# The k-kernel generation of a two-layer attention and state-space block: another hand-written order, an earlier zero fill, a later load and two earlier projections

## The chip, the cores and the metric

The kernel runs on one core of a Trainium2 chip. The metric is the device time of one execution in microseconds (us). A core has five engines with their own instruction streams: PE (TensorE, matrix products), DVE (VectorE), ACT (ScalarE), POOL (GpSimd) and SP (SyncE, which here only issues DMA transfers). Each engine works through its stream in order and waits on semaphores. All DMAs but one are issued from SP, so SP's stream is also an order of transfers.

## The reference, cut to what matters

```python
x = x + A(layernorm(x))      # attention, 32 heads of 16, 8 keys back at distance 2
x = x + B(layernorm(x))      # S4: long convolution with a generated kernel K
x = x + A(layernorm(x))      # the same weights again
x = x + B(layernorm(x))

# A: qkv = x @ wqkv; logits over 8 dilated keys; softmax; o = attn @ v; o @ wo
# B: dt = exp(log_dt); P = exp(dt * (A_re + i A_im) * l), l = 0..2047
#    K = real(sum_n C * P * dt * B)          # 512 x 2048, bf16 positions
#    y = irfft(rfft(u, 4096) * rfft(K, 4096))[:2048] + u * Dskip
```

x is 2048 x 512 in bf16, the state size N is 128. K depends on the inputs alone and is the same in both B layers.

## The kernel before, in words

**Stages.** The program has six stages, each handing over to the next on the engines without a barrier: the generation of K together with the front of the first A layer (`k_gen`, L883, until about 119 us), the rest of the first A layer (`LayerA.core`, L307, until about 209 us), the first B layer by a two-level Fourier transform (`FftB`), the second A layer, the second B layer, and the stores of the output, spread over the last stage.

**`k_gen`.** K is built from powers of z = exp(dt*A). Eleven squarings give z to the power 1, 2, 4, ... 2048; DVE multiplies two sets of tables out of them (`B_t` for coarse positions, `A_t` for fine ones, in four chunks of channels), PE contracts the tables over the 128 states into PSUM, ACT copies them to `kgs`, and SP stores them to `kd_dram` in 48 small DMAs (`k_store`, L1147). Into the gaps goes the front of attention: the statistics of x, its normalisation, its transposes, the projections to q and k, and the first three logit products of block 0. The order of all this is written out by hand: `ORDERK` (L44) is a string of 376 letters, each letter is a list of small closures, and the loop at L1211 calls the next closure of the letter. The tile framework keeps that order on DVE, ACT, PE and SP (`manual_schedule`). The letters that the prediction speaks of:

- s: ACT squares both parts of the current power (L959). i: DVE finishes the next power, in turn `double` (L963) and `differ` (L966).
- b: ACT casts a power into `B_t` (L975) or into the fine table `pow_t` (L973, and its negative at L978). c: SP copies a plane of `pow_t` (L981).
- C: DVE forms the coefficient dt*B*C (eight products). M: DVE builds `B_t` (`bmul`, L995).
- T, U: DVE builds `A_t`, chunks 0 and 2 by T, 1 and 3 by U (L1093). The first U also frees the small buffers of the generation (`stage_two`, L1088), so its copy (L1099) waits for everything that reads them.
- a, l, W, y, z: statistics of x rows (ACT), four small DVE steps per block of x, of which the last (L1056) needs the power -1/2 that POOL makes (W, L1060), then the normalisation on ACT (y, L158) or DVE (z).
- t, e, k, q, K, Q: transposes and projections on PE, their copies out of PSUM on ACT (L1072, L1084). d, E, w, on SP: loads of x blocks 2 and 3, the shifted copies of k (L253), the stores of the twiddle table `w2` (L652).
- p, x: the contraction on PE (L1136), its copy on ACT (L1144). X, Z, g: logit products of block 0 on DVE, their sums on PE, masks.

At the start SP issues the loads of A, B and C, the first block of x, the weights for k and q (`front_w`, L213), the second block of x, and the zero fill of `w2_dram` (`zero`, L645): 4 MB from a 128 x 256 tile of zeros, in pieces of 512 bytes. The fill has to be complete before w2 is stored over it.

**After the letters.** The two `k_store` calls come last in SP's stream of this stage, behind the E copies and the load of the v weights (`load_wv`, L258), and ahead of the loads of the output weights, of Dskip, and of the first shifted copy of v.

**`core` of layer 0.** Nine slots (block 0 from its fourth product on, blocks 1 and 2) each do one product q*k on DVE (`mult`, L289) and its head sums on PE (`lsum`, L298). The projections still missing, 16 of v and 4 of q, are dealt out over the slots at an even rate:

```python
449	            slots = [(0, ft) for ft in range(nprod, NDT)] + [(q, ft) for q in (1, 2) for ft in range(NDT)]
450	            free = 2 if l else 0
451	            per, acc = len(projs) / (len(slots) - free - 0.5), 0.0
```

After v blocks 14 and 15 a shifted copy of v is made by two DMAs (L353, L354), one for the even, one for the odd blocks; x is loaded again behind the second. Then 16 steps follow, each with one weighted sum attn*v: the product on DVE (`pv_mult`, L394), its sum on PE (L407), the output projection (L413). Events hang on these steps (`ev`, L1328): at ("o", n) after step n, at ("p", n) within it. Among them: the load of each half of K from `kd_dram` in 18 DMAs (`k_half_load`, L1305); the four sines of the second twiddle table, each with its store to `g2_dram` (`sines`, L678), which use the buffer `kp` as scratch; `k_half_fix` and `k_part` (L1311, L1315), which copy K into the same `kp`, quarter by quarter, so quarter j of the first half waits until store j has been read out; and the load of w2 (L539).

Of the kernel before, what the change touches and what calls it, by code (L numbers as in the profile page):

```python
# [15 lines left out]
BF16 = mybir.dt.bfloat16  # L16
# [4 lines left out]
P = 128  # L21
# [8 lines left out]
EXP_LN = "natural_log_exp_and_others"  # L30
# [11 lines left out]
DQT = 8  # L42
NQT = DQG // DQT
ORDERK = """  # L44
iCsbisCbiiCbiMsGMiaCCsibCbcGisCMCbaMTibTiasMcbTMiaibbTsMbTaacMcTiMTMaTaiTsbilGTGlilbTWTlGsiibMMy
MMMyaGTyGGbMyGMisMacTtMMiaaaMtdaMaMaGaebMasliMlMqleMWMqialMyMyQMGwqyyMqQbkMkMaMMKtUgkUaUkkUTUaaU
UatUKUppkklkdeUlKxUqqlUpW3UKl3UxQpTUeTkqkqTy3yyyTt3KTTQElqtTxkqlkQxTKpkqkWTKpxkqTlTxTezepzQTpkkU
zUUKkzUKTkkkUtUkTKekkUKtxqKqQUUkpeUqkqUExxpUKUXxUpUxkpQkUEUKUkkxUUkKpxpXkXKUpXXxpZXxZgZx
"""
ORDER0 = """  # L50
KA KD KA KD KA KA KD KA KD KA KD kA KD KA KA kD kA kD kA UA KD UA UA UD UA kD UA
# [111 lines left out]
class LayerA:  # L163
# [143 lines left out]
    def core(self, x_sb, u, lnp, ev=None, nprod=0):  # L307

        tc, nc, lnst, l = self.tc, self.nc, self.lnst, self.layer
# [3 lines left out]
        ev = ev or {}  # L313
# [8 lines left out]
        with ExitStack() as c2:  # L322
            self.prp = c2.enter_context(tc.tile_pool(name=f"a{l}_prod", bufs=2, reuse_waits="tile"))
            big = c2.enter_context(tc.tile_pool(name=f"a{l}_big", bufs=1, reuse_waits="tile"))
            v = big.tile([P, NA + 14, D], BF16, name="v_ext")
# [119 lines left out]
            projs = [(q_proj, 1, ft) for ft in range(NDT)] if 1 not in self.qT else []  # L445
# [2 lines left out]
            projs += [(v_proj, a) for a in vs[6:]]  # L448
            slots = [(0, ft) for ft in range(nprod, NDT)] + [(q, ft) for q in (1, 2) for ft in range(NDT)]
            free = 2 if l else 0  # L450
            per, acc = len(projs) / (len(slots) - free - 0.5), 0.0

            def proj(n):
                nonlocal acc
# [118 lines left out]
def build_b_consts(nc, cpool, tmp, w2_dram):  # L573
# [6 lines left out]
    aidx = iota_f32(nc, tmp, "aidx", 16, step=4096)  # L580
    d4i = iota_f32(nc, tmp, "d4i", 4)
    nc.gpsimd.iota(base[:], pattern=[[16, EQ], [4096, 16]], base=8, channel_multiplier=0)
    zt = tmp.tile([P, 256], BF16, name="w2_zero")
    nc.gpsimd.memset(zt[:], 0.0)
    t_i = tmp.tile([P, 8], I32, name="pk_t")
    nc.vector.tensor_scalar(t_i[:, 0:1], pi_i[:], 63, 2, ALU.bitwise_and, ALU.logical_shift_right)
# [56 lines left out]
                                dmask_m.unsqueeze(1).to_broadcast([P, 32, 4]), ALU.mult)  # L643

    def zero():  # L645
        nc.sync.dma_start(w2_dram.rearrange("p e c -> p (e c)").rearrange("p (n x) -> p n x", x=256),
                          zt[:].unsqueeze(1).to_broadcast([P, P * P // 256, 256]))

    def w2_store():
        for s in range(4):  # L650
# [6 lines left out]
    steps += [lambda nm=nm, t=t: f1_sine(nm, t) for nm, t in zip(("F1c", "F1s"), f1t)]  # L657
    steps += [w2_sine] + [lambda name=name: w_sine(name) for name, offs in wps]
    return C, zero, steps, w2_store, [lambda name=name: w_mask(name) for name, offs in wps]


# [4 lines left out]
def build_g2(nc, tmp, p21, g2_dram, room):  # L666

    s8 = 2.0 * math.pi / 65536 * SIN_SHRINK
    own = tmp.tile([P, 2, 8 * P], I32, name="g2_i")
    gi = [own[:, 0], own[:, 1], *(room[:, (2 + h) * 16 * P:(3 + h) * 16 * P].bitcast(I32) for h in range(2))]  # L670

    def indices(h):
        for k, bias in enumerate((16384.0, 32768.0)):
            g = gi[h][:, k * 4 * P:(k + 1) * 4 * P]
            nc.gpsimd.iota(g.rearrange("p (a m) -> p a m", m=P), pattern=[[8, 4], [128, P]], base=32 * h, channel_multiplier=0)
            nc.gpsimd.tensor_scalar(g, g, p21, bias, ALU.mult, ALU.add)

    def sines(h):  # L678
        gs = room[:, h * 8 * P:(h + 1) * 8 * P]
        nc.scalar.activation(gs, low16(gi[h]), ACT.Sin, scale=s8)  # L680
        nc.sync.dma_start(g2_dram[:, :, h * 4:(h + 1) * 4, :], gs.rearrange("p (k a m) -> p k a m", k=2, a=4))

    return indices, sines
# [199 lines left out]
def k_gen(tc, nc, ident, ins, kd, la, x_v, lnst, b_consts):  # L883
# [4 lines left out]
    with ExitStack() as ctx:  # L888
# [16 lines left out]
        def x_load(b):  # L905
            xb[b] = la.fp.tile([P, 4, D], BF16, name="x_blk")
            nc.sync.dma_start(xb[b][:], x_v[:, b * 4:(b + 1) * 4, :])
# [4 lines left out]
        for name in ("A_im", "A_re", "B_re", "B_im", "C_re", "C_im"):  # L912
            raw[name] = sp.tile([P, 4, N], BF16, name="raw_" + name)
            nc.sync.dma_start(raw[name][:], ins[name].rearrange("(t p) n -> p t n", p=P))
            if name == "A_re":
                x_load(0)
        la.front_w()
        x_load(1)
        C, zero, steps, w2_store, masks = b_consts(sp)
        zero()  # L920
        nc.vector.memset(Bt[:, 0, :, 0, :], 1.0)
        nc.vector.memset(Bt[:, 1, :, 0, :], 0.0)

# [236 lines left out]
        def first_logits():  # L1160
            pr = {}

            def mult(ft):
                if ft == 0:
                    pr[0] = tab[0].tile([P, 2, W, 4, P], BF16, name="A_pr", tag="A_t")
                    pr[1] = tab[0].tile([P, W, 4, P], BF16, name="A2_pr", tag="A_t2")
                la.mult(0, ft, pr[0][:, ft] if ft < 2 else pr[1][:])

            for ft in range(3):
                yield lambda: la.front_ext(3, "dve", ft)  # L1170
                yield lambda: mult(ft)
# [13 lines left out]
        def calls(f, *args):  # L1185
            return [lambda a=a: f(*a) for a in args]

        def chain(*fs):
# [18 lines left out]
            p=calls(product, *((c, j) for c in range(NCH) for j in range(CH // 8))),  # L1207
            x=calls(produced, *((c, j) for c in range(NCH) for j in range(CH // 8))), X=first_logits(), Z=calls(lsum, (0,), (1,), (2,)))
# [15 lines left out]
def k_load(tc, nc, kr, kd, ds_):  # L1224
    l = np.arange(2048, dtype=np.float32)
    m = bf16_round_np(l).astype(np.int64).reshape(128, 16) - 16 * np.arange(128)[:, None]
    nc.sync.dma_start(kr[0:16], kd[0:256, ds_].rearrange("(p a) d -> p a d", a=16))
    n = 1
    for o, (p0, p1, base) in enumerate(((16, 32, 256), (32, 64, 384), (64, 128, 512))):
        s = 2 << o  # L1230
        blk = m[p0:p1]
        assert (blk == blk[0:1]).all() and (blk % s == 0).all()
        row = [int(v) for v in blk[0]]
        np_ = p1 - p0
        q = 16 // s
        runs = []
        for v in range(0, 17, s):
            c = [a for a in range(16) if row[a] == v]
            assert c == list(range(c[0], c[-1] + 1))
            runs.append((v // s, c[0], len(c)))  # L1240
        for (t, a0, cnt) in runs:
            rows = kd[base + t:base + t + (np_ - 1) * q + 1:q, ds_]
            nc.sync.dma_start(kr[p0:p1, a0:a0 + cnt, :],
                                                              rows.unsqueeze(1).to_broadcast([np_, cnt, D // 2]))
            n += 1
# [3 lines left out]
def kernel(  # L1249
# [16 lines left out]
    nc = tc.nc  # L1266
    cpool = ctx.enter_context(tc.tile_pool(name="consts", bufs=1))
    dram = ctx.enter_context(tc.tile_pool(name="dram", bufs=1, space=bass.MemoryType.DRAM))
    w2_dram = dram.tile([P, P, P], BF16, name="w2_dram")
# [16 lines left out]
    la = LayerA(tc, nc, consts, lnst, A_wqkv, A_wo, 0, xnT, 2)  # L1286

    with tc.manual_schedule(engines=MAN):
        C = k_gen(tc, nc, consts["ident"], ins, kd, la, x_v, lnst, lambda sp: build_b_consts(nc, cpool, sp, w2_dram))
# [15 lines left out]
    def k_half_load(h):  # L1305
        hs = slice(h * 256, (h + 1) * 256)
        kr = krp.tile([P, NA, D // 2], BF16, name=f"k_rl{h}")
        k_load(tc, nc, kr, kd, hs)
        krs[h] = kr

    def k_half_fix(h):  # L1311
        kr = krs[h]
        nc.vector.tensor_tensor(kr[0:1, 0, :], kr[0:1, 0, :], dsk[:, h * 256:(h + 1) * 256], ALU.add)

    def k_part(h, j):  # L1315
        cp = nc.scalar.copy if j % 2 == 0 else nc.vector.tensor_copy
        cp(kp[:, h * 64 + j * 16:h * 64 + (j + 1) * 16, :, :],
           krs[h][:, :, j * 64:(j + 1) * 64].rearrange("p a (q r) -> p q a r", r=4))

    def x_load():  # L1320
        for b in range(4):
            nc.sync.dma_start(x_sb[:, b * 4:(b + 1) * 4, :], x_v[:, b * 4:(b + 1) * 4, :])

    with tc.tile_pool(name="ctmp_g2", bufs=1) as g2tmp, tc.manual_schedule(engines=MAN):
        gx, gs = build_g2(nc, g2tmp, C["p21"], g2_dram, kp[:].rearrange("p q a r -> p (q a r)"))
        G = lambda f, h: lambda: f(h)
        K = lambda h, j: lambda: k_part(h, j)
        ev = {("v", 1): [x_load], ("o", 1): [lambda: k_half_load(0)], ("o", 2): [G(gs, 0)], ("o", 4): [lambda: k_half_load(1)],  # L1328
              ("m", 1, 0): [lambda: nc.scalar.preload_act_table_set(EXP_LN)],
              ("m", 0, 3): [G(gx, h) for h in range(4)],  # L1330
              ("p", 3): [G(gs, 1)], ("p", 4): [G(gs, 2)], ("p", 5): [G(gs, 3)], ("o", 5): [lambda: nc.scalar.preload_act_table_set(EXP_LN)],
              ("p", 6): [lambda: k_half_fix(0), K(0, 0)], ("p", 7): [K(0, 1)], ("p", 8): [lambda: la.load_w2(w2_dram), K(0, 2)], ("p", 9): [K(0, 3)],
              ("p", 12): [lambda: k_half_fix(1), K(1, 0)], ("p", 13): [K(1, 1), K(1, 2)], ("p", 14): [K(1, 3)]}
        late = la.core(x_sb, u, lnp, ev, 3)
# [12 lines left out]
    la = LayerA(tc, nc, consts, lnst, A_wqkv, A_wo, 1, xnT, 1)  # L1347
    la.front_w()
    with tc.manual_schedule(engines=MAN):
# [21 lines left out]
        def last(*ops):  # L1371
            def f():
                for op, *ix in ops:
# [6 lines left out]
                     e=lambda ft: la.front_ext(3, "dve", ft))  # L1380
# [5 lines left out]
        ev = {("p", 8): [lambda: la.load_w2(w2_dram)]}  # L1386
# [56 lines left out]
```

## Time and profile before

| what | value |
|---|---|
| median of 6 runs | 439.38 us (437.22 to 442.78) |
| the profiled execution: its own time | 438.89 us |
| the profiled execution: span from first to last instruction | 437.1 us |
| what lies around the span in it | 1.8 us |
| busy over the span: PE, DVE, ACT, POOL | 80%, 90%, 74%, 9% |
| mean granted TensorE clock | 0.992 |
| bytes moved by DMA | 54.17 MB, 124 GB/s over the span |

The page's section on 40 slices (10.9 us each) shows how the load changes:

```profile
PE   2000238899889989989897889999999899998795
DVE  7979999999999999889789868969999999889974
ACT  6988979776355549978899997874655558779862
DMA  7951282123113465490365650680033056224405
```

Each digit is the busy share of a slice in tenths. The first ten slices are `k_gen`: DVE is full from the third slice on, PE only from the seventh. Slices 11 to 19 are the first attention layer, in which both are full. The DMA engines are full in the second slice, which is the zero fill.

### The profile page before, as it was taken

How to read it: one execution, taken by the hardware profiler on the slowest of the kernel's cores; microseconds unless marked ns; L12 is line 12 of the kernel's file. 1: busy time of each engine (PE TensorE's matmuls, PEld its weight loads, DVE VectorE, ACT ScalarE, POOL GpSimd, SP SyncE). 2: the span in 40 equal slices, each digit the busy share in tenths (PEclk: the TensorE clock that was granted, in tenths of full speed). 3: DMA queues.
4: the chain of work that ended last, by engine and by line, in shares of the span. 5: the costliest groups of instructions: out<-in, count | busy, mean ns of one | idle time of the engine just before them, and what ended most of it. 6: DMA issues, size and time to landing. Idle time of an engine off the chain costs nothing.

```text
span 437.1 us, 12711 instructions
## 1 busy us (share of the span) xinstructions
PE 349.9 (80%) x5459; PEld 264.2 (60%) x5502; DVE 392.9 (90%) x549; ACT 323.2 (74%) x544; POOL 40.9 (9%) x46
## 2 busy tenths in 40 slices
PE   2000238899889989989897889999999899998795
PEld 1000115666745657867787888556557687867694
DVE  7979999999999999889789868969999999889974
ACT  6988979776355549978899997874655558779862
POOL 2002020110394000000500000000000020000000
PEclk9999999999989989999999999999999999999999
DMA  7951282123113465490365650680033056224405
GB/s 217 335 145 24 60 84 61 26 61 88 24 23 106 116 219 161 125 363 7 111 238 205 249 173 1 175 260 2 2 85 86 1 200 241 92 99 145 149 25 169
DMA packets 71499, 54.17 MB, mean 124 GB/s; under 512 B 36781, under 2 KB 61970, under 8 KB 70162
## 3 DMA queue, kind: packets, MB, share of 16 engines
q1 hardware_dynamic: 71298, 53.22, 40.7%
q8 instruction: 43, 0.70, 0.7%
q10 hardware_dynamic: 144, 0.13, 0.2%
q14 instruction: 14, 0.11, 0.1%
HBM read 30.28 MB, written 13.24 MB: 100 GB/s over the span
## 4 chain that ended last, share of the span: by engine, by line
PE 50%; DVE 18%; ACT 17%; DMA 8%; issue 3%; SPq 3%; POOL 1%; DVEq 0%; ACTq 0%; POOLq 0%
PE po L407 9%; PE pq L348 7%; PE L L302 5%; PE pq L419 5%; ACT a1s L725 4%; DVE A_t L984 4%; PE pq L185 4%; PE pp L242 3%; PE pb L808 3%; PE pb L809 2%; DVE B_t L984 2%; DVE pav L399 2%; PE pk L1136 2%; DVE t L783 2%; ACT ub L795 2%
## 5 line engine op out<-in xcount | busy, mean ns | idle before, releaser
L399 DVE TENSOR_TENSOR pav<-attn,v_ext 128x4096 bf16<-128x4096 bf16 x32 | 72.8, 2282 | 0.4 <-DMA v_ext<-v_ext 0.3
L295 DVE TENSOR_TENSOR prod<-qT,kT_ext 128x4096 bf16<-128x4096 bf16 x29 | 66.6, 2313 | 0.4 <-PE L L302 0.2
L407 PEld LDWEIGHTS <-pav 128*128 128x128 bf16 x1024 | 59.0, 98 | 10.1 <-DVE pav L399 5.4
L407 PE MATMUL po<-ident,pav 128*128 128x128 bf16 x1024 | 62.6, 219 | 2.4 <-DVE pav L399 2.3
L984 DVE TENSOR_TENSOR A_t<-A_t,pow_t 128x1024 bf16<-128x1024 bf16 (+4 forms) x46 | 38.2, 869 | 2.6 <-DMA pow_t<-pow_t 2.5
L1069 PE MATMUL pt<-ident,x_blk 128*128 128x128 bf16 x64 | 6.9, 253 | 38.9 <-ACT x_blk L158 38.9
L1079 PE MATMUL pp<-xnT,kT_ext 128*128 128x512 bf16 x88 | 25.3, 414 | 12.9 <-ACT xnT L1072 9.5
L350 ACT CAST v_ext<-pq 128x512 bf16<-128x512 f32 x32 | 18.7, 587 | 22.0 <-PE pq L348 18.2
L795 ACT CAST ub<-pb 128x1024 bf16<-128x1024 f32 x32 | 32.9, 1087 | 2.6 <-DVE t L783 2.5
L302 PEld LDWEIGHTS <-prod 128*128 128x128 bf16 x928 | 27.4, 96 | 9.3 <-DVE prod L295 2.7
L808 PE MATMUL pb<-Wp,t 128*128 128x128 bf16 x256 | 30.1, 219 | 3.0 <-ACT ub L795 2.6
L348 PE MATMUL pq<-wv,xnT 128*128 128x512 bf16 x119 | 31.6, 393 | 0.6 <-issue 0.2
L743 PE MATMUL pb<-a1s,w_sb 128*128 128x64 bf16 x768 | 27.1, 193 | 5.7 <-ACT ub L795 3.3
L1069 PEld LDWEIGHTS <-x_blk 128*128 128x128 bf16 x64 | 5.2, 114 | 41.9 <-ACT x_blk L158 40.2
L419 PE MATMUL pq<-wop,oT 128*128 128x512 bf16 x110 | 29.6, 383 | 1.0
L725 ACT CAST a1s<-pb 128x1024 bf16<-128x1024 f32 x30 | 29.2, 1076 | 1.3 <-PE pb L736 1.3
L809 PE MATMUL pb<-WpJ,t 128*128 128x128 bf16 x256 | 30.1, 219 | 0.0
L410 ACT CAST oT<-po 128x512 bf16<-128x512 f32 x32 | 18.5, 579 | 15.4 <-PE po L407 15.3
L743 PEld LDWEIGHTS <-w_sb 128*128 128x128 bf16 x768 | 24.7, 98 | 8.1 <-issue 7.0
L302 PE MATMUL L<-ind,prod 128*128 128x8 bf16 x928 | 27.5, 166 | 2.0 <-DVE prod L295 1.9
L809 PEld LDWEIGHTS <-t 128*128 128x128 bf16 x256 | 24.9, 97 | 3.8 <-issue 2.7
L1136 PE MATMUL pk<-B_t,A_t 128*64 128x84 bf16 (+1 forms) x512 | 23.6, 201 | 2.0 <-DVE A_t L984 1.9
(226 smaller groups left out, 849.8 us busy)
## 6 DMA issues: line engine op xcount, KB each, us to landing
w_sb<-w_dram SPq DMA_DIRECT2D x8, 1024.0 KB, 8.7
w_dram<-w_zero SPq DMA_DIRECT2D x1, 4096.0 KB
kf_ring<-kf_dram SPq DMA_DIRECT2D x13, 256.0 KB, 3.7
kf_ring<-kf_dram SPq DMA_DIRECT2D x26, 128.0 KB, 3.6
v_ext<-v_ext SPq DMA_DIRECT2D x4, 784.0 KB, 6.1
x_blk<-in_A_x_dram SPq DMA_DIRECT2D x4, 512.0 KB
kT_ext<-in_A_wqkv_dram SPq DMA_DIRECT2D x4, 512.0 KB, 5.4
x_sb<-in_A_x_dram SPq DMA_DIRECT2D x4, 512.0 KB, 7.3
```

The costliest lines, as they stand in the source:

```text
L295: nc.vector.tensor_tensor(pr, self.qT[q][:, ft].unsqueeze(1).to_broadcast([P, W, 4, P]), kap, ALU.mult)
L302: self.nc.tensor.matmul(L[:, al, w, ft * 8:(ft + 1) * 8], lhsT=pr[:, w, al, :], rhs=self.c["ind8"][:], start=(ft == 0 and w == 0 and al % ...
L348: nc.tensor.matmul(pp[:], lhsT=xnT[:, dt, a * P:(a + 1) * P], rhs=wv[:, dt, :], start=(dt == 0), stop=(dt == NDT - 1))
L399: nc.vector.tensor_tensor(pv[:], attn[:, n % 4].unsqueeze(2).to_broadcast([P, W, DH, H]), vap, ALU.mult)
L407: nc.tensor.matmul(po[:, ft, :], lhsT=pvf[:, w, ft * P:(ft + 1) * P], rhs=ident[:], start=(w == 0 and ft == 0), stop=(w == W - 1), skip_gr ...
L419: nc.tensor.matmul(pw[:], lhsT=oT[:, ftp, :], rhs=wo[:, ftp, :], start=False, stop=(ftp == NDT - 1))
L725: (self.nc.scalar.copy if eng == "act" else self.nc.vector.tensor_copy)(dst, src)
L743: nc.tensor.matmul(p2[:, j, :], lhsT=self.w2[:, ec * EC + j, :], rhs=a1s[:, ec * EC + j, :], start=True, stop=True)
L795: nc.scalar.copy(ub[:], p2)
L808: nc.tensor.matmul(p3[:, j, :], lhsT=t1[:, dql, :], rhs=wp_r, start=True, stop=False)
L809: nc.tensor.matmul(p3[:, j, :], lhsT=t2[:, dql, :], rhs=wpj_r, start=False, stop=True)
L984: return lambda: nc.vector.tensor_tensor(*args)
```

## The change

Five edits, all in the first two stages; nothing of the computation changes.

```diff
-            per, acc = len(projs) / (len(slots) - free - 0.5), 0.0
+            lead = 0 if l else 2
+            per, acc = (len(projs) - lead) / (len(slots) - free - 0.5), float(lead)
...
-    zt = tmp.tile([P, 256], BF16, name="w2_zero")
+    zt = tmp.tile([P, 1024], BF16, name="w2_zero")
...
-        nc.sync.dma_start(w2_dram.rearrange("p e c -> p (e c)").rearrange("p (n x) -> p n x", x=256),
-                          zt[:].unsqueeze(1).to_broadcast([P, P * P // 256, 256]))
+        nc.sync.dma_start(w2_dram.rearrange("p e c -> p (e c)").rearrange("p (n x) -> p n x", x=1024),
+                          zt[:].unsqueeze(1).to_broadcast([P, P * P // 1024, 1024]))
...
-        la.front_w()
-        x_load(1)
         C, zero, steps, w2_store, masks = b_consts(sp)
         zero()
+        x_load(1)
+        la.front_w()
...
-        ev = {("v", 1): [x_load], ("o", 1): [lambda: k_half_load(0)], ("o", 2): [G(gs, 0)], ("o", 4): [lambda: k_half_load(1)],
+        ev = {("v", 1): [x_load], ("o", 1): [lambda: k_half_load(0)], ("o", 2): [G(gs, 0)], 
...
-              ("p", 3): [G(gs, 1)], ("p", 4): [G(gs, 2)], ("p", 5): [G(gs, 3)], ("o", 5): [lambda: nc.scalar.preload_act_table_set(EXP_LN)],
+              ("p", 3): [G(gs, 1)], ("p", 4): [G(gs, 2)], ("p", 5): [G(gs, 3), lambda: k_half_load(1)], ("o", 5): [lambda: nc.scalar.preload_act_table_set(EXP_LN)],
```

1. `ORDERK` is replaced by another order of the same 376 letters:

```diff
-iCsbisCbiiCbiMsGMiaCCsibCbcGisCMCbaMTibTiasMcbTMiaibbTsMbTaacMcTiMTMaTaiTsbilGTGlilbTWTlGsiibMMy
-MMMyaGTyGGbMyGMisMacTtMMiaaaMtdaMaMaGaebMasliMlMqleMWMqialMyMyQMGwqyyMqQbkMkMaMMKtUgkUaUkkUTUaaU
-UatUKUppkklkdeUlKxUqqlUpW3UKl3UxQpTUeTkqkqTy3yyyTt3KTTQElqtTxkqlkQxTKpkqkWTKpxkqTlTxTezepzQTpkkU
-zUUKkzUKTkkkUtUkTKekkUKtxqKqQUUkpeUqkqUExxpUKUXxUpUxkpQkUEUKUkkxUUkKpxpXkXKUpXXxpZXxZgZx
+sbiCiCiCsiaCCbbMsaMiaiMbCiCGbMCcsMTaGiMsbiibacTTsMbTMiibTMsacTiTiaTbTcMalbTGlsiliTbsTbWbliMyMyyy
+aitMMsMMbMiMteGadGaGTGMMiMaGGbaMeaacMMqMaGqsiqMaaQMqMGMlMlMlWMaTlkTkMQkMyykiyyKtawtMqKkaqMbkUgpa
+UUUUpaaUUxQxpedekUpUlKUllUkUKxqqW3UlTqUTyTqQUQkkTyk3TkKTT3kxKpkxpyTT3KypxTkltpkTqetKeklqkQTkkKUT
+WUUTTKkxlqkUKqxpkgUUzxQUzUUzUzppkxtUKteepkkExEUUkUxUUEKUkUkpUkXKUKxqpkqxkXXUQpXpXKZXZxxZ
```

2. The zero fill is written in pieces of 2 KB (16 pieces per partition instead of 64), from a tile four times as wide that POOL sets to zero.
3. SP issues the fill ahead of the second x block and of the two weight loads; before, it stood behind the three.
4. The load of the second half of K moves from after step 4 to within step 5, behind the store of the fourth sine.
5. In layer 0 the even rate starts with two projections in hand: `acc` begins at 2 and `per` falls from 20/8.5 to 18/8.5, so the first slot issues four v projections instead of two and the last two stay in the last slot. Layer 1 keeps its rate.

More of the change, by code (lines that the diff above doesn't have):

```diff
@@ L44 @@
 ORDERK = """
-iCsbisCbiiCbiMsGMiaCCsibCbcGisCMCbaMTibTiasMcbTMiaibbTsMbTaacMcTiMTMaTaiTsbilGTGlilbTWTlGsiibMMy
-MMMyaGTyGGbMyGMisMacTtMMiaaaMtdaMaMaGaebMasliMlMqleMWMqialMyMyQMGwqyyMqQbkMkMaMMKtUgkUaUkkUTUaaU
-UatUKUppkklkdeUlKxUqqlUpW3UKl3UxQpTUeTkqkqTy3yyyTt3KTTQElqtTxkqlkQxTKpkqkWTKpxkqTlTxTezepzQTpkkU
-zUUKkzUKTkkkUtUkTKekkUKtxqKqQUUkpeUqkqUExxpUKUXxUpUxkpQkUEUKUkkxUUkKpxpXkXKUpXXxpZXxZgZx
+sbiCiCiCsiaCCbbMsaMiaiMbCiCGbMCcsMTaGiMsbiibacTTsMbMTiibMTsacTiTiaTbTcMalbTGlsiliTbsTbWbliMyMyyy
+aitMMsMMbMiMteGadGaGTGMMiMaGGbaMeaacMMqMaGqsiqMaaQMqMGMlMlMlWMaTlkTkMQkMyykiyyKtawtMqKkaqMbkUgpa
+UUUUpaaUUxQxpedekUpUlKUllUkUKxqqW3UlTqUTyTqQUQkkTyk3TkKTT3kxKpkxpyTT3KypxTkltpkTqetKeklqkQTkkKUT
+WUUTTKkxlqkUKqxpkgUUzxQUzUUzUzppkxtUKteepkkExEUUkUxUUEKUkUkpUkXKUKxqpkqxkXXUQpXpXKZXZxxZ
 """
```

## The prediction

> **What bounds the kernel now.** I read busy shares first, then a table by stage, then DVE's waits, then SP's timeline. The table of stages (start:end, length, busy time and instructions of PE, PEld, DVE, ACT, POOL, TensorE clock, DMA share, GB/s):
>
> ```profile
> 12.00:30.00 18.00, 0.00 (x0) 0.00 (x0) 15.50 (x29) 16.21 (x24) 0.00 (x0) 1.00 0.88 267
> 30.00:60.00 30.00, 3.44 (x18) 1.98 (x19) 29.09 (x48) 27.93 (x57) 2.98 (x1) 1.00 0.30 50
> 60.00:90.00 30.00, 24.71 (x272) 15.72 (x276) 28.22 (x56) 23.41 (x44) 5.76 (x3) 1.00 0.31 53
> 90.00:110.00 20.00, 19.32 (x276) 13.80 (x278) 19.86 (x29) 13.71 (x21) 0.00 (x0) 1.00 0.34 74
> 120.00:150.00 30.00, 27.64 (x379) 16.30 (x382) 29.04 (x21) 15.98 (x28) 15.68 (x12) 0.94 0.26 63
> ```
>
> DVE is full from 12 us to 150 us, so up to there the time is DVE's work plus DVE's waits. No edit removes DVE work: each letter and product is still there. Only waits can be won. DVE's waits until 125 us (total, times, longest):
>
> ```profile
> DVE A_t L984 <- DMA pow_t<-pow_t: 2.5, 1, 2.5
> DVE ln_nb L1056 <- POOL ln_rstd L1060: 1.8, 2, 0.9
> ...
> DVE A_t L1099 <- ACT B_t L975: 0.7, 1, 0.7
> ```
>
> and those of 125 to 215 us that touch the change:
>
> ```profile
> DVE k_perm L1317 <- DMA g_dram<-k_perm: 2.6, 1, 2.6
> ...
> DVE attn L389 <- ACT rs L383: 0.6, 1, 0.6
> ...
> DVE pav L399 <- DMA v_ext<-v_ext: 0.3, 1, 0.3
> DVE prod L295 <- PE L L302: 0.2, 1, 0.2
> ```
>
> These are the whole field: 2.46 + 0.91 + 0.91 + 0.73 = 5.01 us in the generation, 0.59 + 0.24 + 0.33 = 1.16 us in `core`, 2.57 us at the fourth quarter of K. The chain of waits runs through three of them: the copy of `pow_t` issued at 21.17, POOL's power at 40.21 and 60.74, the store of `g_dram` at 182.32. SP's stream explains what comes later (start, duration, line):
>
> ```profile
> 99.53 0.49 SPq L261 DMA_DIRECT2D wv<-in_A_wqkv_dram  x1
> 100.88 32.34 SPq L1158 DMA_DIRECT2D kd_dram<-kgs  x48
> 133.33 1.35 SPq L268 DMA_DIRECT2D wop<-in_A_wo_dram  x2
> ...
> 138.58 0.66 SPq L353 DMA_DIRECT2D v_ext<-v_ext  x1
> 139.28 0.95 SPq L354 DMA_DIRECT2D v_ext<-v_ext  x1
> ...
> 172.67 9.55 SPq L1243 DMA_DIRECT2D k_rl<-kd_dram  x17
> 182.32 1.00 SPq L681 DMA_DIRECT2D g_dram<-k_perm  x1
> 183.43 2.50 SPq L544 DMA_DIRECT2D w_sb<-w_dram  x4
> ```
>
> The 48 stores of K take SP 32.3 us without a gap (0.67 each), and everything for v stands behind them. At 182.32 the store of the fourth sine leaves, although ACT finished that sine at 174.66: SP was busy with the second K half.
>
> **What the Trainium skill says.** "DMA: Bandwidth & Descriptors", § "Why small descriptors are slow (HBM only)": a packet costs a fixed 3 cycles or so beside its 32-byte beats. The trace agrees in direction: the fill in 512-byte pieces runs at 348 GB/s (window 14 to 16 us), the w2 load in 8 KB rows at 422 (192 to 194 us). Same page, § "Queues, rings and completion order": each engine has a ring per queue row; within a queue its descriptors start in order (§ "Two DMAs through the same engine are not ordered"). The trace agrees: the first `pow_t` copy, behind the fill, landed 5.6 us after issue, the later ones in 2.3. "SBUF — State Buffer", § "Who interferes with whom": DVE and GpSimd share a port pair that one locks. POOL's four powers took 2.98, 2.59, 1.82 and 1.34 us beside a busy DVE; the trace doesn't show the cause, so I keep these durations and their spread.
>
> **Part by part. 1, the new order.** I replayed the new letters with durations from the rows.
> - *First multiply by `pow_t` (L984).* Before, 12.1 us of DVE work lay between 12.04 and it, and it had to wait until 26.89. In the new order 14.56 us lie ahead of it (8 to 9 more instructions of 0.6), so DVE arrives at 26.6. The copy lands when SP's ring has drained to it: the bytes ahead are the same, so at 26.8 with the fill as before, or near 25.4 with a faster one (below). Wait 0 to 0.2: gain 2.3 to 2.46.
> - *POOL's powers.* Ahead of the last small step (L1056) stands one more `differ` (0.60) in block 0: 0.91 becomes 0.31. In block 1 it is 2.8 us instead of 1.8: 0.91 becomes 0. At POOL's fastest both vanish; were it 0.6 us slower than the row, they would be 0.9 and 0.5. Gain 1.5 (0.4 to 1.8).
> - *L1099, the copy after `stage_two`.* It waits for the last ACT cast of the powers. From the third block's step on, ACT has 4 x 0.72 + 0.47 + 0.62 + 0.47 + 0.62 + 0.95 = 6.0 us, DVE 0.1 + 2.2 + 5 x 0.6 = 5.3. Wait 0.7, as before: gain 0.
> - Moved steps with slack: the other `pow_t` copies (0.8 and 3 us before their readers), the w2 stores (landed about 1 us before `A_t` needs the buffer), K's transposes.
>
> Sum 5.01 - 1.16 = 3.85 us (bounds 1.5 to 4.6). The lower bound holds one new wait of 2 us that the replay missed.
>
> **2 and 3, the fill.** Same 4 MB, a quarter of the pieces. If a packet is beats + 3 cycles, 19/16 of overhead falls to 67/64: 348 becomes 395 GB/s, 10.6 us instead of 12.05 (an estimate from the page named first). Nothing but the first copy waits for it. POOL's memset grows from 0.30 to about 1.2 us, at 2.6, while POOL is idle and SP reaches the fill at about 5.7; the x block behind it (first used at 44.85) and the k and q weights (57.34) have over 15 us of cover. Cost 0. Without the new order this saves up to 1.4; with it 0.1.
>
> **5, two v projections up.** PE idles 1.9 us until 122.06 because the first product of `core` is not ready; two projections of about 0.85 us fill that. The same work is missing later: the backlog that makes DVE wait for the softmax (0.59) and for the logits' buffer (0.24) shrinks by 1.7 us. Casts of v cannot start before 120.27, since their buffer shares space with `A_pr`, so the first head sum may slip 0.6; DVE's next product, 2.3 us, hides it.
> So DVE would reach its first attn*v, at 147.06 now, 3.85 + 0.83 = 4.7 us earlier, at 142.4. But this reads shifted v, which lands 5.8 us after an issue at 138.58/139.28: at 145.1. SP's stream in front of it starts with the E copies and `wv`, which follow the transposes that K letters finish at about 99.5 in the new order, and its 48 stores still need 0.67 each: 100.8 + 48 x 0.67 + 4.4 (weights, Dskip, first v copy) = 137.5, not 4.7 earlier. The v casts themselves are done by then, and the shift no longer waits the 1.06 us for v14's cast as it did. Shifted v lands at about 144.1: gain at this point 147.06 - 144.1 = 3.0, and DVE stalls 1.7. Each us of SP's start is one us here.
> Behind it, the second shifted v and x come no later than DVE: 0.33 more.
>
> **4, the second K half behind the sine.** Removed: 18 issues (10.2 us of SP) ahead of the store. The store leaves at about 174.7, lands 3.9 later at 178.6, 5 us before DVE's fourth quarter at 184.2: gain 2.57. Moved: K's second half is issued until about 185.9, its last pieces land up to 8.2 us later at 194, and its first reader is at 195.99; the w2 load moves from 183.43 to about 186, lands at 195 to 197, and is read first at 215.2. Cost 0, with 2 us of cover for the K half: that margin is the thinnest here, and each us over costs one. PE has 22 us of work in the same stretch and doesn't bind.
>
> **Sum.** 3.0 + 0.33 + 2.57 = 5.9 us. The profiled execution took 438.89 (span 437.1 + 1.8 around it): 433.0. The median is 0.49 above it: 433.5 us. After 209 us nothing changes, so the gain is carried to the end.
>
> **The rivals.**
> - *SP caps more, or a small new wait stays in the generation.* For: SP's stream has no gap, and my replay knows waits only at row precision. The gain is 1.5 to 4.4: 435 to 437.9, in the main 436.2.
> - *SP caps nothing.* If K's letters let SP start 1.7 us earlier, shifted v comes in time: 4.7 + 0.33 + 2.57 = 7.6, 431.8. For: K letters stand earlier in the last line. Against: the last E copies need the transposes of the last q and k.
> - *It doesn't do what it says.* The waits move, not vanish: DVE's 2.5 us at `pow_t` comes back at another copy, or the K half is late by 2 us. 438 to 440. Against: the wait at `g_dram` has a plain cause and goes alone.
> - *Slower: the fill becomes slow.* The 2 KB pieces read one partition row 16 times; the trace has no such pattern. The one wait is at L984: DVE arrives at 26.6, the copy lands when the fill does, and each us after that is a us of the whole. From 348 GB/s down to 233 (18 us of fill) the 5.9 us are gone; at 150 GB/s (28 us) it is 16 us late: about 449. Against: larger pieces were faster in every window (422 over 348).
>
> **How the numbers follow.** Main 0.52 (own range 432.0 to 435.3), SP or a small wait 0.22, no cap 0.12, no effect 0.08, slow fill 0.06. One per cent is 4.4 us, about what a measurement of this kernel can tell from no change: the bound is 435.0. Below it: nearly all of main (0.50), no cap (0.12), a little of the second: 0.64. Within 1%: 0.28. Slower: the slow fill and a part of no effect, 0.08. The range 431.0 to 437.8 holds main, no cap and most of the second: 0.85.
>
> **What would show it.** Right: no wait of DVE on the `pow_t` copy near 26.7; one wait of about 0.3 on POOL; L1099 still at 0.7; a new DVE wait of about 1.5 us on `v_ext` at the first attn*v; no wait on `g_dram`; SP's stores of K from 100.8 and the shift at 137.5. Wrong: another start of SP's stores, a fill under 300 GB/s, DVE waiting on `k_rl` at 196 less the gain, or a new releaser in DVE's list ahead of 119 us.

## The result, and the profile after

| | before | changed |
|---|---|---|
| median | 439.46 us (37 runs) | 435.78 us (18 runs, 433.16 to 438.04) |
| the profiled execution: own time, span | 438.89, 437.1 us | 435.95, 434.2 us |
| ratio of the changed kernel to the one before | | 0.9910, 95% interval 0.9892 to 0.9929 |

The changed kernel is 3.7 us faster, where 5.9 were forecast; a second measurement, beside other runs of the kernel before, gave 0.9924 (0.9903 to 0.9945). So the direction and the range held, and the size was too large by more than half of what came. Two of the 22 runs of the second measurement, and one of experiment 1, were in a slower state of the chip and are left out. The views below show where the difference lies.

DVE's waits of the changed kernel, until 125 us (waiter, releaser: total, times, longest):

```profile
DVE ln_nb L1057 <- POOL ln_rstd L1061: 1.8, 2, 0.9
DVE A_t L1100 <- ACT B_t L976: 0.9, 1, 0.9
...
DVE mx L360 <- PE L L285: 0.6, 1, 0.6
```

and from 125 to 215 us:

```profile
DVE a1s L726 <- PE pb L737: 3.7, 1, 3.7
DVE pav L399 <- DMA v_ext<-v_ext: 1.9, 1, 1.9
```

(Lines behind about 450 stand one further down than before.) Four waits are gone, as forecast: 2.5 us on the copy of `pow_t`, 2.6 on the store of `g_dram`, and the 0.6 (L389) and 0.2 (L295) in `core`. Four lines are not as forecast. POOL's 1.8 is exactly what it was. L1100 has 0.9 instead of 0.7. There is a new 0.6 on the first logits of block 0 (L360). At the seam to the transform (L726, near 206 us) DVE waits 3.7 in one piece, where it had 1.0 and 1.6 with work between. The 1.9 on `v_ext` was forecast, at 1.7, but that the sizes meet is luck: DVE came there at 144.97 instead of 142.4, and shifted v at 146.8 instead of 144.1, both 2.6 to 2.7 us late. SP's timeline (start, duration):

```profile
102.14 0.50 SPq L261 DMA_DIRECT2D wv<-in_A_wqkv_dram  x1
102.69 32.56 SPq L1159 DMA_DIRECT2D kd_dram<-kgs  x48
...
139.14 0.67 SPq L353 DMA_DIRECT2D v_ext<-v_ext  x1
139.85 0.94 SPq L354 DMA_DIRECT2D v_ext<-v_ext  x1
...
164.96 7.47 SPq L682 DMA_DIRECT2D g_dram<-k_perm  x4
...
173.14 9.51 SPq L1244 DMA_DIRECT2D k_rl<-kd_dram  x17
```

SP begins the stores of K 1.8 us later than before, though DVE is 2 us ahead (at the first logit product of block 0, 108.6 instead of 110.6); the shifted v is issued 0.6 us later and arrives at 146.8, which is 7.0 us after the issue of its second copy (139.85). In experiment 2, where DVE waits for the same copy, it was 5.9. The four stores of the second twiddle now leave one after the other, ahead of the second K half, as the edit says.

Because the whole time scatters by 4 us between executions of one kernel, I follow two marks in each profile: the start of the first attn*v (L399), and the start of the last small step of the layer norm at the seam (L148). Their places are read from DVE's timeline.

| kernel | first attn*v | seam (L148) | between | end of span |
|---|---|---|---|---|
| before | 147.06 | 213.24 | 66.18 | 437.1 |
| changed | 146.91 | 210.79 | 63.88 | 434.2 |
| changed, measured again (experiment 9) | 145.01 | 208.89 | 63.88 | 434.2 |

The second execution of the same kernel is 1.9 us ahead at both marks and ends at the same time: it lost its lead in the second attention layer, where it was 1.75 us ahead at 327 us and 0.1 at 373. In that layer its TensorE clock fell to 0.50 from 339 to 341 us, and 32 matmuls at 337.8 took 3.08 us instead of 1.96; DVE then waited 0.22 us for PE and 0.59 for ACT where the first execution did not wait. How much of the 1.7 comes from the dip is not shown: in the first execution the clock was 0.50 from 147 to 153 us, and the stretch between the marks took 63.88 all the same. Behind the seam, where no edit of this document changes anything, the fourteen profiles need 223.4 to 227.2 us. So the marks tell more than one end.

### The profile page after: what moved, and what is told of

Read it like the earlier page. It is cut to its first block, busy times and chain, and to the rows that moved or that the text cites. A ratio compares the mean times of both kernels' runs of the same rounds, so it can differ in the third digit from the quotient of the medians.

```text
span 434.2 us, 12709 instructions
## 1 busy us (share of the span) xinstructions
PE 352.6 (81%) x5459; PEld 265.1 (61%) x5502; DVE 393.3 (91%) x549; ACT 322.8 (74%) x544; POOL 51.6 (12%) x46
## 4 chain that ended last, share of the span: by engine, by line
PE 42%; ACT 13%; DVE 10%; DMA 5%; SPq 3%; issue 2%; DVEq 0%; ACTq 0%
PE po L407 8%; PE pq L348 5%; PE L L302 4%; ACT a1s L726 4%; PE pq L419 4%; DVE pav L399 4%; PE pq L185 4%; PE pp L242 3%; PE pb L809 3%; PE pb L810 2%; DVE t L784 2%; ACT ub L796 2%; DMA v_ext<-v_ext 2%; PE pb L825 1%; PE pb L826 1%
## 5 line engine op out<-in xcount | busy, mean ns | idle before, releaser
L399 DVE TENSOR_TENSOR pav<-attn,v_ext 128x4096 bf16<-128x4096 bf16 x32 | 72.7, 2281 | 2.0 <-DMA v_ext<-v_ext 1.9
L407 PEld LDWEIGHTS <-pav 128*128 128x128 bf16 x1024 | 60.3, 99 | 12.6 <-DVE pav L399 8.4
L407 PE MATMUL po<-ident,pav 128*128 128x128 bf16 x1024 | 64.2, 222 | 3.7 <-DVE pav L399 3.6
L295 DVE TENSOR_TENSOR prod<-qT,kT_ext 128x4096 bf16<-128x4096 bf16 x29 | 66.5, 2314 | 0.2
L1080 PE MATMUL pp<-xnT,kT_ext 128*128 128x512 bf16 x87 | 26.6, 430 | 12.5 <-ACT xnT L1073 7.9
L348 PE MATMUL pq<-wv,xnT 128*128 128x512 bf16 x119 | 30.1, 379 | 1.1 <-ACT v_ext L350 0.7
L726 ACT CAST a1s<-pb 128x1024 bf16<-128x1024 f32 x30 | 29.3, 1077 | 1.3 <-PE pb L737 1.3
L726 DVE CAST a1s<-pb 128x1024 bf16<-128x1024 f32 x18 | 21.5, 1219 | 6.2 <-PE pb L737 5.9
```

The source lines that it names most:

```text
L295: nc.vector.tensor_tensor(pr, self.qT[q][:, ft].unsqueeze(1).to_broadcast([P, W, 4, P]), kap, ALU.mult)
L348: nc.tensor.matmul(pp[:], lhsT=xnT[:, dt, a * P:(a + 1) * P], rhs=wv[:, dt, :], start=(dt == 0), stop=(dt == NDT - 1))
L399: nc.vector.tensor_tensor(pv[:], attn[:, n % 4].unsqueeze(2).to_broadcast([P, W, DH, H]), vap, ALU.mult)
L407: nc.tensor.matmul(po[:, ft, :], lhsT=pvf[:, w, ft * P:(ft + 1) * P], rhs=ident[:], start=(w == 0 and ft == 0), stop=(w == W - 1), skip_gr ...
L726: (self.nc.scalar.copy if eng == "act" else self.nc.vector.tensor_copy)(dst, src)
```

## The experiments

**1. The second K half alone.** The kernel before, with

```diff
-("o", 4): [lambda: k_half_load(1)],
-("p", 5): [G(gs, 3)],
+("p", 5): [G(gs, 3), lambda: k_half_load(1)],
```

> The kernel before with one edit: the second K half behind the store of the fourth sine. Theory A (DVE frees 2.57 us, but PE is full behind it: the 32 matmuls of K's first transform block, which filled PE's gap at 187.8 before, come after the last output projection, and cost 1 us at the seam): gain 1.6 us, ratio 0.9964, DVE's wait on g_dram gone, its wait on L736 near 206 us grown to 3.5 or more. Theory B (parts simply add): gain 2.57, ratio 0.9941, no longer wait at the seam.

Ratio 0.9972 (0.9955 to 0.9989), by that 1.2 us faster; 64.25 us between the marks instead of 66.18, so 1.9 of the 2.57. PE's first transform matmul on K, in the timeline of the kernel before and of this one:

```profile
187.76 0.24 PE L736 MATMUL pb<-F1c,k_perm 128*64 128x128 bf16 x1
```

```profile
205.68 0.24 PE L736 MATMUL pb<-F1c,k_perm 128*64 128x128 bf16 x1
```

In the kernel before, this block of 32 matmuls stood in PE's order inside the attention layer, and ran in the gap that DVE's pause at the fourth quarter of K (until 186.8) left on PE. With the edit it stands behind the last output projection. The framework chose that place; that it did so because the pause is gone is inferred. In all eleven profiles that have this edit it comes last, and DVE waits 3.65 us there; in the three without it (before, 2 and 12) it comes at 184 to 188, and the waits are 0.98 and 1.59. Theory A holds in its place and near its size.

**2. The new order alone**, with the old fill and everything else as before.

> The kernel before with one edit: the new order of the letters, old fill. Theory A (SP's stream decides when shifted v comes; with the new letters SP begins the stores of K at 102 us or later): the wait on pow_t at L984 falls from 2.5 to under 0.4, SP begins the stores at 102 to 103, the shifted copy of v is issued at 139 or later, DVE waits 1.5 to 2.5 us for it, and the time is within 0.4 us of before (ratio 0.999 to 1.001). Theory B (the order's own gain counts): 2 to 2.4 us faster, ratio 0.995.

Ratio 0.9938 (0.9917 to 0.9959), by that 2.7 us faster, near theory B (2 to 2.4). Theory A was right about L984 (no wait) and about the start of SP's stores (102.27), and wrong about the rest: the shift is issued at 138.45, shifted v landed at 145.1, and DVE waited 1.07 us for it, not 1.5 to 2.5. First attn*v at 145.12, the seam at 210.10. So the order's gain does come through, but for the part that SP takes. Of the 3.14 us at the seam 1.94 stand at the first attn*v; the other 1.2 came between the marks, half of it where DVE's pause at the fourth quarter of K took 1.98 instead of 2.57.

**3. All but the order**: the changed kernel with the old letters.

> The changed kernel with the old letters: fill first in 2 KB pieces, half load moved, two projections up. Theory A (the faster and earlier fill alone brings the copy of pow_t in time, and with the old letters SP's stores start at about 98.5, so that SP doesn't cap): wait at L984 under 0.5, shifted v in time, gain 2.3 + 0.8 + 0.3 + 2.6 - 1.0 = 5.0 us, 434.4, about 1.4 us faster than the changed kernel. Theory B (the order is what removes the wait; the fill is worth 1.4 at most): 1 us or more slower than the changed kernel, 436.5 to 437.

Ratio 0.9920 (0.9897 to 0.9943), the same as the changed kernel within the intervals: beside the other four edits the new order shows no gain of its own. The edits of the fill alone halve the wait, on DVE's timeline:

```profile
25.62 0.29 DVE L985 TENSOR_TENSOR A_t<-A_t,pow_t 128x256 bf16<-128x256 bf16 x1 [1.22 <-DMA pow_t<-pow_t]
```

Before it was 2.46. SP's stores begin at 99.61 here, the shift goes out at 135.71, and no wait on `v_ext` is left; first attn*v at 144.91, the seam at 208.79. With the old letters and half of the wait still there it is about where the new letters come at their best (144.6 to 145.0 in 4, 7 and 9). Theory A was right about SP, and wrong that the wait would be under 0.5.

**4. Output weights later.** In the changed kernel the four loads of the output weights go behind the first shifted copy of v.

```diff
-            self.load_wo(big)
+            wo_issue = self.load_wo(big)
+            if l:
+                wo_issue()
+            else:
+                ev["v", 0] = [wo_issue]
```

> The changed kernel with the four loads of the output weights moved from ahead of the first shifted copy of v to behind it. Theory A (SP's stream caps the gain of the generation): the shift is issued 2.5 us earlier, at about 136.6, DVE's wait of 1.94 us on v_ext goes, 1.0 to 1.9 us faster than the changed kernel (433.9 to 434.8). Theory B (SP isn't the cap; v's casts or the transfer are): the shift is issued when it was, no change, 435.8.

The shift is issued at 135.59, the wait on `v_ext` is gone, first attn*v 144.58, the seam 208.46: 2.3 us ahead of the changed kernel's first profile, as theory A has it. But the ratio is 0.9924 (0.9907 to 0.9942): the gain of 1.0 to 1.9 us that it forecast for the time did not come. In its profile 1.8 of the 2.3 went in the transform behind, where DVE waited 1.77 us for a transfer of K's spectrum (`kf_nat`) at 252.9; other kernels ahead by as much (3, 8) had no such wait. Experiment 9, the changed kernel again, shows another reason:

> The changed kernel once more, beside the other runs of this call. Theory A (the stores of K take SP 30.8 to 32.9 us from one execution to the next, and what is over goes into DVE's wait for shifted v): its first attn*v lies between 144.6 and 147, the times spread over 3 us or more. Ratio to before near 0.991.

Its 48 stores took SP 31.67 us instead of 32.56, so that the second copy for shifted v was issued at 139.09 instead of 139.85; shifted v was there by 145.0, and DVE didn't wait. The times ran from 433.62 to 440.05 us. Theory A names only a part: 0.76 us of the difference is the issue, and at least 1.0 is the transfer, which took 7.0 us in the first profile and 5.9 at most here. Why it was slower there is open. The wait is real but not in every execution, and what experiment 4 takes away wasn't always there.

**5 and 6. POOL's power.** Experiment 5 puts more DVE work between the power and its reader:

```diff
-WbliMyMyyy
+WbiMlyMyyy
...
-WMaTlkTkM
+WMaTTlkkM
```

> The changed kernel with two letters moved, so that more DVE work lies between POOL's power and the DVE step that needs it (one i and one M more in block 0, 1.55 us; one T more in block 1, 2.3 us). Theory A (POOL cannot read while DVE runs instructions with two SBUF inputs back to back; its power ends some 0.87 us after a pause or a lucky boundary): DVE's two waits on ln_rstd stay near 0.9 each, or vanish only where POOL got in at a boundary, and POOL's durations grow to 4 us and more. Theory B (POOL's power takes up to 3.6 us, whatever DVE does): both waits vanish, POOL's durations stay under 3.6. Time within 0.5 us of the changed kernel in A, 0 to 1.8 faster in B.

Experiment 6 lets POOL do the step behind the power, so that DVE never pauses:

```diff
-nc.vector.scalar_tensor_tensor(nb[:], mean, ms, rstd[:], ALU.mult, ALU.mult)
+nc.gpsimd.tensor_scalar(nb[:], mean, ms, None, ALU.mult)
+nc.gpsimd.tensor_tensor(nb[:], nb[:], rstd[:], ALU.mult)
```

> The changed kernel with the step after the power (nb = mean * rstd) made on POOL instead of DVE, so that DVE never pauses for POOL. Theory A (POOL is kept out by DVE's two-input work): POOL's power and the two steps behind it stretch to 5 us or more in blocks 0 and 1, ACT waits for them, and little or nothing is won. Theory B (fixed durations): power 3.6 + two steps of 1 us at most, ACT has slack, DVE's 1.8 us are won at the end of the generation.

POOL's timeline, the powers of blocks 0 and 1 (start, duration), of the changed kernel, of 5, and of 6:

```profile
37.26 3.58 POOL L1061 TENSOR_TENSOR ln_rstd<-ln_rstd,ln_mh 128x4 f32<-128x4 f32 x1 [33.74 <-DVE ln_rstd L1056]
58.79 3.58 POOL L1061 TENSOR_TENSOR ln_rstd<-ln_rstd,ln_mh 128x4 f32<-128x4 f32 x1 [17.95 <-DVE ln_rstd L1056]
```

```profile
37.25 5.05 POOL L1061 TENSOR_TENSOR ln_rstd<-ln_rstd,ln_mh 128x4 f32<-128x4 f32 x1 [33.73 <-DVE ln_rstd L1056]
59.41 5.79 POOL L1061 TENSOR_TENSOR ln_rstd<-ln_rstd,ln_mh 128x4 f32<-128x4 f32 x1 [17.11 <-DVE ln_rstd L1056]
```

```profile
36.95 10.03 POOL L1067 TENSOR_TENSOR ln_rstd<-ln_rstd,ln_mh 128x4 f32<-128x4 f32 x1 [1.48 <-DVE ln_rstd L1056]
64.17 8.82 POOL L1067 TENSOR_TENSOR ln_rstd<-ln_rstd,ln_mh 128x4 f32<-128x4 f32 x1 [1.62 <-DVE ln_rstd L1056]
```

In these two blocks the same instruction on 4 columns takes 2.6 to 10 us over the runs, and grows by what DVE does. Each time it ends about 0.9 us after DVE stops: in 5, DVE's waits are 0.91 and 0.90 as before, behind 1.5 and 2.3 us more work. In 6 DVE works until 46.07 without a gap, then waits for ACT, which waits for POOL; the power ends at 46.98. In its second block DVE stops at 72.10 and the power ends at 72.99.

```profile
52.74 0.69 DVE L985 TENSOR_TENSOR B_t<-B_t 128x1024 bf16<-128x1024 bf16 x1 [6.67 <-ACT B_t L976]
```

Experiment 5 is slower than the changed kernel (0.9981, interval 0.9958 to 1.0005 to before; the moved letters also make L1100 wait 3.1 us), and 6 is 1.45% slower than before (1.0145, 1.0086 to 1.0203). Theory B falls. The Trainium skill, "SBUF — State Buffer", § "Who interferes with whom", says that a DVE instruction with two SBUF inputs contends with a GpSimd instruction that reads SBUF, and that this is an exclusive lock on the ports that the two share. DVE's instructions around here are two-input ones, and the traces agree; they add that a chain of such instructions keeps POOL out over most boundaries between them. That it is the second input that matters was not varied here; what the runs show is that the power doesn't end while DVE's chain goes on.

**7 and 12. Does PE bind?** Eight matmuls of 512 columns more in step 9 (1.76 us at 0.22 each), in the changed kernel and in the one before:

```diff
                 pv_sum(rows[n])
+                if l == 0 and n == 9:
+                    self.warm(pq_tile(), 8, wo[:, 0, :])
```

> The changed kernel with 8 matmuls of 512 columns more in step 9 of the first attention layer (1.76 us of PE, their result unused). Theory A (PE is co-bound from 150 us to the seam, so that 1 us of the 2.57 was lost to it): 1.2 to 1.8 us slower than the changed kernel, all of it at the seam (DVE's wait on L737 near 206 us grows by it). Theory B (PE doesn't bind there): within 0.4 us of it.

> The kernel before with the 8 matmuls of experiment 7 in step 9. Theory A (PE had room there before, in the gap of 2.57 us at the fourth quarter of K): no more than 0.4 us from before at the seam. Theory B (PE was bound there before as well): 0.8 us or more later at the seam, as in experiment 7.

Between the marks 7 takes 64.76 us instead of 63.88, 0.88 more, and 12 takes 65.93 instead of 66.18, none more; the ratios to before are 0.9915 (0.9879 to 0.9950) and 1.0000 (0.9976 to 1.0024). Half of the added matmuls found room in the changed kernel, all of them before, as theory A of 12 has it. So PE is near its limit there since the pause is gone, but not past it: 7 lies between its two theories. Nor is its loss where its theory A put it: the wait at the seam is 3.65 as before, and 0.50 us came at L389 (187.9 us) and 0.29 at L101 (200.8). Whether the place of the 32 matmuls or the fullness of PE makes the 1.1 us at the seam isn't separated.

**8, 10 and 11. The loads behind the copies.** Experiment 3 left 1.2 us at L984 with 1.5 MB of loads between the fill and the first copy. Experiment 8 takes them from there:

```diff
         zero()
-        x_load(1)
-        la.front_w()
...
             nc.sync.dma_start(Pw[:, :, k, 0, :], Pw[:, :, k, 1, :])
+            if k == 1:
+                x_load(1)
+            if k == 3:
+                la.front_w()
```

> Experiment 3 (all but the order) with the second x block and the k and q weights issued behind the copies of pow_t. Theory A (the remaining wait of 1.2 us at L984 is the ring: 1.5 MB of loads between the fill and the first copy): no wait at L984, 1.0 to 1.2 us faster than experiment 3, 434.1. Theory B (the copy's own issue at 21 us or the fill's end sets it): wait stays above 0.8, no change. Theory C (the gain arrives at the seam, but the chain of K's spectrum behind it takes it): milestones 1.2 us earlier until 208 us, time as in experiment 3.

Experiment 10 goes back to pieces of 512 bytes in it, experiment 11 adds the edit of experiment 4 to it.

> Experiment 8 with the fill in 512-byte pieces again. Theory A (the place of the loads in the ring is what matters; the fill has 1.5 us of cover): the fill runs at 350 GB/s instead of 395 and ends 1.3 to 1.5 us later, the wait at L984 stays under 0.5, no difference to experiment 8 (ratio 0.985 to 0.988). Theory B (the size of the pieces is what matters): the wait at L984 comes back with 1 us or more, ratio 0.989 or above.

> Experiment 8 with the output weights behind the first shifted copy of v as well. Theory A (with the old letters SP is early enough, so that v doesn't wait): first attn*v and time as in experiment 8, ratio 0.984 to 0.987, no wait on v_ext. Theory B (SP still caps in some executions): 0.5 us or more faster than experiment 8.

DVE's timeline in experiment 8 shows the multiply without a wait, 2.6 us earlier than before and after:

```profile
24.32 0.28 DVE L987 TENSOR_TENSOR A_t<-A_t,pow_t 128x256 bf16<-128x256 bf16 x1
```

| | first attn*v | seam | median | ratio to before |
|---|---|---|---|---|
| 8 | 143.61 | 207.49 | 434.42 | 0.9853 (0.9812 to 0.9893) |
| 10, 512-byte pieces | 143.84 | 207.72 | 434.66 | 0.9893 (0.9856 to 0.9931) |
| 11, output weights late | 144.00 | 207.87 | 434.04 | 0.9874 (0.9837 to 0.9911) |

The three are one kernel as far as these runs can tell, with neither a wait at L984 nor on `v_ext` at the first attn*v. Theory A holds for the waits in all three: what was left of the copy's delay came from its place in the ring. In 10 the fill runs at 294 GB/s, slower than before (348) and than expected (350), and still nothing waits for it. The ratios of 10 and 11 lie a little above what theory A gave (up to 0.988 and 0.987); that of 10 is the number of its theory B, but the wait that theory B needs isn't there. These kernels, with the old letters, are 1.1 to 1.5% faster than before, and at the seam 1.0 to 3.3 us ahead of the two profiles of the changed kernel. Measured beside each other, 11 (0.9837 to 0.9911) and the changed kernel (experiment 9, 0.9903 to 0.9945) have intervals that just overlap, but the runs themselves hardly do: all six of 11 took 432.79 to 435.27 us, and 17 of the 20 of the changed kernel took longer than any of them. So it is ahead at the end too. The new letters with the loads behind the copies were not run.

## Why the prediction was right in sign and too large

- **First multiply by `pow_t`: right.** Forecast gain 2.3 to 2.46; the wait is gone. The estimate for the fill, 395 GB/s from the cost per packet ("DMA: Bandwidth & Descriptors", § "Why small descriptors are slow (HBM only)"), met the trace, but in part by luck:

```profile
9.00:14.00 5.00, 0.96 (x9) 0.69 (x7) 3.75 (x7) 4.92 (x8) 0.00 (x0) 1.00 1.04 394
```

  The estimate starts from 348, the rate of the 512-byte pieces behind the loads. Ahead of the loads they ran at 294 in experiment 10, and the same working from 294 would give 333. Experiment 3 measured what fill and place are worth under the old letters: 1.24 of the 2.46 ("up to 1.4" in the prediction). What the prediction did not ask is whether the loads could also go behind the copy; experiment 8 shows that this is the other half.
- **POOL's powers: this step failed.** It reckoned with a fixed duration under more DVE work and forecast 1.5 us; 0.0 came. The prediction quoted the shared port pair, and then kept "these durations and their spread". With what it had it could have seen more: two powers of 2.98 and 2.59 us with the same DVE wait of 0.91. A wait that does not change with the work ahead of it begins when that work ends. Under the new letters both powers took 3.58 us and the waits stayed 0.91 and 0.90; experiments 5 and 6 show why.
- **L1099: 0 forecast, 0.17 lost.**
- **Two projections up: waits right, sum too large.** The 0.59 and the 0.24 are gone here and in 3, and both stand in 2, which lacks the edit; 0.63 came up at L360 in the changed kernel, and neither in 2 nor in 3, so it belongs to the two edits together. That leaves 0.2 instead of 0.83 in this combination.
- **SP: the mechanism right, its terms mis-sized.** Stores of K at 102.7 instead of 100.8: the new letters finish the last copies of k later than my replay had them. Shifted v at 146.8 instead of 144.1 in the first profile, by 145.0 in the second. Of the 3.0 forecast at the first attn*v came 0.15 and 2.05. The prediction treated the stores' 0.67 us apiece and the 5.8 us to landing as fixed; the 48 took 30.8 to 32.9 us over the profiles, and the landing 5.9 to 7.0, more together than the stall of 1.7 at stake. In the second profile SP doesn't limit at all: DVE itself comes at 145.0, where the prediction had it at 142.4, and POOL (1.5), L360 (0.63) and L1099 (0.17) make 2.3 of these 2.6 us.
- **The second K half: right for the wait, wrong for its worth.** 2.57 gone, K's second half and w2 in time. "PE has 22 us of work in the same stretch and doesn't bind" is the step that failed: at the seam DVE now stands idle for 0.35 + 3.65 = 4.0 us, before for 0.35 + 0.98 + 1.59 = 2.92, so 1.1 of the gain went there; whether by PE's fullness or by the new place of the 32 matmuls is open. The pause had been of use: 32 matmuls of the next stage ran in the gap that it left on PE.

Together, with the second profile, whose DVE met no delay from v: at the seam 4.35 came where 5.9 were forecast, 0.95 short at the first attn*v and 0.6 between the marks (2.3 instead of 2.9). In the first profile 2.45 came. The rival of a smaller gain, with SP capping more and a small wait staying in the generation, is the nearer description, and 435 to 437.9 holds both medians. The rival of a slow fill found nothing; that SP caps nothing held in single executions, without the 7.6 us that it promised. The end of the span came 2.9 us earlier in both profiles, so that the gain at the seam was not carried to the end as it stood there: the first execution ends with 0.45 us more than it had at the seam, the second with 1.45 less.

## What to carry to other kernels

Before work is put ahead of a wait to hide it, ask whether the thing waited for can run beside that work; if the wait stays the same length in all its occurrences, it can't. A transfer that is late in a ring is helped first by moving what stands ahead of it and has slack, which here, with the faster fill, removed the same wait as a new order of 376 steps and left the kernel at least as fast. And a pause that is removed may have been the place where the next stage's work ran: look at what the other engines do in it before its length is booked as a gain.

## What the hardware showed that I had not expected

- A POOL operation on 128 x 4 elements took between 1.34 and 10.03 us, by what DVE ran beside it.
- With 4 MB in the ring ahead, SP's issues of the next loads took 2.3 to 2.8 us each, where most take 0.5 to 0.7 otherwise.
- The fill in 512-byte pieces ran at 348 GB/s behind the loads (14 to 16 us) and at 294 ahead of them (10 to 16 us, experiment 10).
- The same SBUF to SBUF copy of v landed 5.9 us after its issue in one profile (experiment 2) and 7.0 in another (the changed kernel).
